# Deferring the table build, adding buffers, moving work between engines and re-ordering a linear-attention, Fourier-mix and MLP kernel

## The chip, the cores and the metric

The kernel runs on one core of one Trainium2 chip. The metric is the device time of one execution in microseconds (us). The kernel before took 268.16 us (median of three executions, 267.31 to 1089.49; the long one is a first execution and is not used; a fourth, 265.46, was taken with the changed kernel, and the median of the three fast ones is the 267.3 of the tables). Most fast executions of one kernel agree within about 1%. In a slow one the time is over 1.5% above the fastest of the same kernel.

Names: TensorE (PE in the profile, PEld for its weight loads), VectorE (DVE), ScalarE (ACT), GpSimd (POOL). Sync (SP) issues most DMAs. "Span" is the length of the profiled execution, some 2 us less than its time.

## The reference, cut to what matters

```python
B, H, S, D = 4, 8, 768, 48                    # d_model = H*D = 384, hidden = 1536
for t in range(S):                            # linear attention with a decaying state
    cur = einsum('bhd,bhe->bhde', u * k_t, v_t)
    y_t = einsum('bhd,bhde->bhe', r_t, state + cur)
    state = w_t[..., None] * state + einsum('bhd,bhe->bhde', k_t, v_t)
x = y, heads merged to (B, S, 384)
mixed = real(fft(fft(x, axis=1), axis=2))     # Fourier mix over both axes
u = x + mixed
un = (u - mean(u)) / sqrt(var(u) + 1e-6)
out = u + maximum(un @ w_ch1, 0) @ w_ch2      # two dense layers, the "experts" of this text
```

## The kernel before

The sequence is cut into six chunks of 128 positions per batch, 24 in all. Every chunk goes through Ln of the decay, matmuls for the running sums, Exp, products, transposes and matmuls, and lands in `x`. A "fold" on VectorE makes even and odd halves of `x`. The Fourier mix of a batch is matmuls of the folded `x` with cosine and sine tables, which the kernel builds itself, and then with a second table (`dtm`, `dtp`). After the mix come normalisation and the experts: `unt` x `w1`, relu to `ht`, then `ht` x `w2`.

No instruction stream is written by hand. Each operation is recorded with its engine, a duration in ns and a priority key. A list scheduler in Python then fixes the order of each engine's instructions. The order is static, so a wrong duration in the model gives another order on the chip.

```python
    def op(self, eng, dur, fn, r=(), w=(), key=None, sem=None, nbytes=0): ...   # cut
    # schedule(): of all ready operations, the one with the least (start, key, idx) goes next
    ...
    NIN = 3                                        # input buffers, 2 of most chunk buffers
    ...
        for i in range(2):                         # small_constants()
            op("dve", 600, fill(RH[i][:, :, :], 0.0), w=[("RH", i)])
            op("pool", 600, fill(XF[i][:, :, :], 0.0), w=[...])     # the whole of xf
        op("dve", 140, ts(MSK[:, :], CI[:, :], 0.0, None, ALU.is_gt), r=["CI"], w=["MSK"])
    ...
        for q in range(NC // 2):                   # seq_tables(): two scratch buffers in turn
            i = (q + 1) % 2
            ...                                    # range reduction on VectorE
            op("act", 420, act(SS[:, q, :], TF[i][:, :], ACTF.Sin, scale=sc), r=[("TF", i)], w=[("SS", q)])
            op("act", 420, act(CS[:, q, :], TG[i][:, :], ACTF.Sin, scale=-sc, bias=BHPI[:, :]),
               r=[("TG", i), "BHPI"], w=[("CS", q)])
    ...
        # attention(): the first use of Ln waits for the table set that has Ln and Exp
        op("act", 420, act(L[:, :, 0:D], wt[:, :, :], ACTF.Ln), r=["ACTT", ("in", "w", i3)], w=[("LB", i2)])
    ...
        op("dve", 270, tt(xf[:, c, 0:193], xb[:, c, 0:193], xb[:, c, 384:191:-1], ALU.add), ...)   # fold
        op("dve", 270, tt(xf[:, c, 321:512], xb[:, c, 1:192], xb[:, c, 383:192:-1], ALU.subtract), ...)
    ...
            op("dve", 270, ts(un[:, :], uf[:, kb, :], agg[:, kb, 0:1], None, ALU.subtract), ...)   # mix()
    ...
                if j % 3 == 2: ...                 # a third of the relus on VectorE, the rest on ScalarE
    ...
    T0, P = 30.0, 44.0                             # key windows: one for all the work of a batch
    def win(b):
        return (0.0, T0) if b == 0 else (T0 + (b - 1) * P, T0 + b * P)
    small_constants()
    seq_tables()
    dm_tables()
    op("act", 1300, lambda e: e.preload_act_table_set("natural_log_exp_and_others"),
       r=[("SS", 2), ("CS", 2), "DTM0", "TS", "DTM2"], w=["ACTT"])
```

## Time and profile before

| | before |
|---|---|
| time, median of the fast runs | 267.3 us |
| span of the profiled execution | 264.3 us |
| first TensorE work | 31.8 us |
| first expert matmul (`unt` x `w1`) | 90.0 us |
| from there to the end | 174.3 us |
| VectorE busy in all | 205.2 us |

The page of the profile gives busy time by engine, the span in 40 slices of 6.6 us (each digit is the busy share in tenths, 9 is 90% or more) and the chain of work that ended last, followed back from the end:

```profile
PE 200.9 (76%) x1776; PEld 125.3 (47%) x1776; DVE 205.2 (78%) x420; ACT 134.5 (51%) x291; POOL 108.6 (41%) x115
...
PE   0000197786785599999977899999778999969995
...
DVE  8999559368999996956899988568999774596232
...
DMA  6999496199792455522577853235410100100102
...
PE 45%; DVE 34%; SPq 8%; ACT 7%; DMA 2%; issue 2%; DVEq 0%; ACTq 0%
```

TensorE does nothing for almost five slices. After that neither engine is full: the chain changes between TensorE (45%) and VectorE (34%), so neither alone bounds the kernel. There is also a dip in the TensorE row four slices from the end.

The same in stretches, from the per-stretch busy times (start:end in us, length, busy us of each engine with its number of instructions, then granted TensorE clock, DMA share, GB/s):

```profile
0.00:31.80 31.80, 0.00 (x0) 0.00 (x0) 28.19 (x70) 9.56 (x16) 19.25 (x27) 1.00 0.92 158
31.80:72.00 40.20, 31.52 (x305) 21.25 (x305) 28.04 (x48) 26.09 (x56) 20.72 (x22) 0.83 0.76 149
72.00:90.00 18.00, 11.66 (x111) 6.50 (x112) 18.00 (x37) 9.79 (x24) 12.95 (x13) 1.00 0.52 102
90.00:264.30 174.30, 157.75 (x1361) 97.59 (x1361) 130.96 (x267) 89.03 (x197) 55.69 (x55) 1.00 0.34 78
```

Why TensorE waits is seen in the timeline (start, length, engine, line, operation, and in brackets how long the engine idled before and what released it):

```profile
2.00 2.65 POOL L386 MEMSET xf<- 128x3072 bf16 x1
...
2.50 2.23 DVE L379 TENSOR_SCALAR msk<-ci 128x128 bf16<-128x128 f32 x1
...
29.86 1.28 ACT L738 ACT_TABLE_LOAD   x1
31.23 0.94 ACT L389 ACTIVATE lb<-in_w 128x384 bf16<-128x384 f32 x2
...
31.81 0.50 PE L517 MATMUL bank<-lb,msk 128*128 128x384 bf16 x1 [31.81 <-ACT lb L389]
...
237.07 3.10 PE L696 MATMUL bank<-unt,w 128*128 128x384 bf16 x18 [0.58 <-ACT unt L677]
```

The first Ln (`lb`) stands behind the Sin evaluations and a table load, and TensorE waits 31.81 us for it. The last batch's experts start at 237.07, after a stretch in which its Fourier mix and normalisation ran alone. The `msk` comparison of 128 columns took 2.23 us beside a GpSimd memset of `xf` that took 2.65.

The groups by shape give the fold pieces and the mean subtraction (count, then busy us, mean ns of one, and idle time of the engine before them):

```profile
L375 DVE TENSOR_TENSOR xf<-x 128x191 bf16<-128x191 f32 x24 | 17.7, 739 | 0.0
...
L379 DVE TENSOR_SCALAR un<-uf,agg 128x384 bf16<-128x384 f32 x24 | 13.2, 552 | 0.0
...
L375 DVE TENSOR_TENSOR xf<-x 128x193 bf16<-128x193 f32 x24 | 10.3, 431 | 0.4
```

### The profile page before, as it was taken

How to read it: one execution, taken by the hardware profiler on the slowest of the kernel's cores; microseconds unless marked ns; L12 is line 12 of the kernel's file. 1: busy time of each engine (PE TensorE's matmuls, PEld its weight loads, DVE VectorE, ACT ScalarE, POOL GpSimd, SP SyncE). 2: the span in 40 equal slices, each digit the busy share in tenths (PEclk: the TensorE clock that was granted, in tenths of full speed). 3: DMA queues.
4: the chain of work that ended last, by engine and by line, in shares of the span. 5: the costliest groups of instructions: out<-in, count | busy, mean ns of one | idle time of the engine just before them, and what ended most of it. 6: DMA issues, size and time to landing. Idle time of an engine off the chain costs nothing.

```text
span 264.3 us, 4663 instructions
## 1 busy us (share of the span) xinstructions
PE 200.9 (76%) x1776; PEld 125.3 (47%) x1776; DVE 205.2 (78%) x420; ACT 134.5 (51%) x291; POOL 108.6 (41%) x115
## 2 busy tenths in 40 slices
PE   0000197786785599999977899999778999969995
PEld 0000165453543256665543566655435666536562
DVE  8999559368999996956899988568999774596232
ACT  1024584575673571745677717456767163227140
POOL 9940642358696458412264774122644200000000
PEclk9999999568899999999999999999999999999999
DMA  6999496199792455522577853235410100100102
GB/s 127 188 196 194 86 216 124 34 176 186 151 198 51 83 116 128 116 60 83 105 144 139 167 132 74 60 83 99 92 30 2 60 32 30 60 2 0 61 32 89
DMA packets 105478, 26.45 MB, mean 100 GB/s; under 512 B 100336, under 2 KB 105072, under 8 KB 105456
## 3 DMA queue, kind: packets, MB, share of 16 engines
q1 hardware_dynamic: 103440, 23.80, 42.7%
q0 software_dynamic: 2016, 2.36, 5.3%
q8 instruction: 14, 0.23, 0.4%
q14 instruction: 8, 0.07, 0.1%
HBM read 23.79 MB, written 4.72 MB: 108 GB/s over the span
## 4 chain that ended last, share of the span: by engine, by line
PE 45%; DVE 34%; SPq 8%; ACT 7%; DMA 2%; issue 2%; DVEq 0%; ACTq 0%
PE bank L715 16%; PE bank L696 11%; SPq L398 8%; DVE xf L375 6%; DVE ah L581 5%; DVE rh L375 5%; PE bank L639 4%; DVE bst L661 4%; DVE uf L657 4%; PE bank L577 4%; DVE un L379 3%; DVE x L614 3%; DMA in_v<-in_v_dram 2%; PE bank L558 2%; PE bank L606 2%
## 5 line engine op out<-in xcount | busy, mean ns | idle before, releaser
L696 PE MATMUL bank<-unt,w 128*128 128x384 bf16 x288 | 53.5, 326 | 1.5 <-ACT unt L677 1.0
L715 PE MATMUL bank<-w,ht 128*128 128x384 bf16 x288 | 51.7, 326 | 0.3 <-DVE ht L701 0.3
L705 ACT ACTIVATE ht<-bank 128x384 bf16<-128x384 f32 x64 | 31.5, 493 | 23.7 <-PE bank L696 23.6
L375 POOL TENSOR_TENSOR vtd<-in_v,dc 128x384 f32<-128x384 f32 x24 | 21.0, 876 | 54.0 <-DVE x L614 29.5
L715 PEld LDWEIGHTS bank<-w,ht 128*128 128x128 bf16 x288 | 27.1, 98 | 17.3 <-issue 1.3
L696 PEld LDWEIGHTS bank<-unt,w 128*128 128x128 bf16 x288 | 26.1, 98 | 17.2 <-ACT ht L705 1.0
L517 PE MATMUL bank<-lb,msk 128*128 128x384 bf16 x24 | 9.1, 380 | 33.1 <-ACT lb L389 32.8
L581 DVE TENSOR_TENSOR ah<-bank,msk 128x512 bf16<-128x512 f32 x48 | 31.1, 681 | 2.3 <-PE bank L577 2.2
L567 ACT ACTIVATE rtb<-bank 128x1024 bf16<-128x1024 bf16 x24 | 24.6, 1025 | 15.0 <-PE bank L558 15.0
L375 POOL TENSOR_TENSOR rk<-in_r,in_k 128x384 f32<-128x384 f32 x24 | 25.3, 1054 | 15.1 <-DMA in_r<-in_r_dram 14.7
L720 DVE SCALAR_TENSOR_TENSOR osb<-bank,rstd,uf 128x384 f32<-128x384 f32 x24 | 14.8, 615 | 21.1 <-PE bank L715 20.9
L375 POOL TENSOR_TENSOR rku<-rk,ub 128x384 f32<-128x384 f32 x24 | 26.3, 1099 | 0.3
L375 DVE TENSOR_TENSOR xf<-x 128x193 bf16<-128x193 f32 (+1 forms) x48 | 26.0, 585 | 0.4
L375 POOL TENSOR_TENSOR kh<-in_k,e_1 128x384 bf16<-128x384 f32 x12 | 13.1, 1090 | 24.3 <-ACT e_1 L625 11.4
L701 DVE TENSOR_SCALAR ht<-bank 128x384 bf16<-128x384 f32 x32 | 17.6, 550 | 6.8 <-PE bank L696 6.4
L389 ACT ACTIVATE vb<-in_v 128x384 bf16<-128x384 f32 x24 | 12.5, 521 | 15.7 <-PE bank L609 13.1
L577 PE MATMUL bank<-rtb,ktb 128*128 128x256 bf16 x96 | 16.6, 293 | 3.4 <-ACT ktb L569 1.7
L558 PE MATMUL bank<-idb,rh 128*128 128x128 bf16 x192 | 17.4, 246 | 1.9 <-DVE rh L375 1.8
L517 PEld LDWEIGHTS bank<-lb,msk 128*128 128x128 bf16 x24 | 2.5, 105 | 34.3 <-ACT lb L389 33.1
L569 ACT ACTIVATE ktb<-bank 128x512 bf16<-128x512 bf16 x24 | 14.3, 594 | 7.3 <-PE bank L564 7.1
L599 DVE TENSOR_TENSOR st<-bank,we 128x384 bf16<-128x384 f32 x20 | 11.0, 550 | 8.6 <-PE bank L594 8.4
L677 ACT ACTIVATE unt<-bank 128x384 bf16<-128x384 bf16 x24 | 11.8, 491 | 11.3 <-PE bank L672 11.2
(102 smaller groups left out, 409.9 us busy)
## 6 DMA issues: line engine op xcount, KB each, us to landing
in_w<-in_w_dram SPq DMA_DIRECT2D x24, 192.0 KB, 3.5
in_k<-in_k_dram SPq DMA_DIRECT2D x24, 192.0 KB, 3.6
in_r<-in_r_dram SPq DMA_DIRECT2D x24, 192.0 KB, 3.2
in_v<-in_v_dram SPq DMA_DIRECT2D x24, 192.0 KB, 3.1
out_dram<-osb SPq DMA_DIRECT2D x24, 192.0 KB, 1.9
w<-in_moe_w_ch_dram POOLq DMA_DIRECT2D x6, 384.0 KB, 9.5
ub<-in_u_dram SPq DMA_DIRECT2D x1, 192.0 KB, 3.7
```

Of the source, the lines that this page charges most:

```text
L375: return lambda e: e.tensor_tensor(out=o, in0=a, in1=b, op=f)
L398: return e.dma_start(INB[n][i][:, :, :], src[n][b, :, c * CH:(c + 1) * CH, :].rearrange("h t d -> t h d"))
L558: ins = e.transpose(psb(trr)[:, 128 * h:128 * h + 128], rflat[:, o0:o0 + 128], IDB[:, :])
L567: op("act", 910, lambda e: e.activation(rT[:, :, :].rearrange("p h t -> p (h t)"), psb(trr)[:, :], ACTF.Copy), r=[trr], w=[("RTB", i2)])
L569: op("act", 480, lambda e: e.activation(kT[:, :, :].rearrange("p h t -> p (h t)"), psb(trk)[:, 0:512], ACTF.Copy), r=[trk], w=[("KTB", i2)])
L577: ins = e.matmul(ps(ta)[:, 256 * x:256 * x + 256], kT[:, q, :], rT[:, 2 * q:2 * q + 2, :].rearrange("p h t -> p (h t)"))
L581: op("dve", 600, lambda e, hf=hf, ta=ta: e.tensor_tensor(out=ah[:, 4 * hf:4 * hf + 4, :], in0=ps(ta)[:, :].rearrange("p (h t) -> p h t", t ...
L696: ins = e.matmul(ps(t)[:, 0:384], W1[:, m, 128 * j:128 * j + 128], unt[:, m, :], start=(m == 0), stop=(m == NM - 1))
L701: op("dve", 480, lambda e, j=j, t=t, ht=ht: e.tensor_scalar(out=ht[:, j, :], in0=ps(t)[:, 0:384], scalar1=0.0, scalar2=None, op0=ALU.max), ...
L705: op("act", 380, lambda e, j=j, t=t, ht=ht: e.activation(ht[:, j, :], ps(t)[:, 0:384], ACTF.Relu), r=[t], w=[("HT", q % 2, j)])
L715: ins = e.matmul(ps(t)[:, 0:DM], ht[:, j, 128 * x:128 * x + 128], W2[:, j, :], start=(j == 0), stop=(j == NJ - 1))
L720: op("dve", 480, lambda e, kb=kb, t=t, o=o: e.scalar_tensor_tensor(out=o[:, :], in0=ps(t)[:, 0:DM], scalar=rstd[:, kb:kb + 1], in1=uf[:, k ...
```

## The change

The intent: let attention start at once and build the tables beside it, with all nine Sin evaluations in one visit to the Sin table set (three table loads in all; before had two). Give the scheduler more buffers, take work off VectorE, and give it new keys and durations that are nearer to those measured. The fold pieces are also laid out so that they start at even columns. Cut to its core:

```diff
-    NIN = 3
+    NIN = 5
+    NB = 3                                        # chunk buffers, 2 before; vb and vtd 4, 3 before
-        op("pool", 600, fill(XF[i][:, :, :], 0.0), ...)
+        op("pool", 400, fill(XF[i][:, :, 0:64], 0.0), ...)          # only the padding
+        op("pool", 400, fill(XF[i][:, :, 446:512], 0.0), ...)
+    def tables():
+        sins = []
+        ...                                        # same arithmetic on VectorE, one buffer per result
+        def all_sins(e):
+            for f in sins:
+                ins = f(e)
+            e.preload_act_table_set("natural_log_exp_and_others")
+            return ins
+        op("act", 8000, all_sins, r=[...], w=["DTM0", "DTM1", "DTM2"] + [...])
     def weights():
-            op("pool", 1000, ..., w=[("W1", q)], ...)
+            op("pool", 1000, ..., r=[("in", "v", 2)], w=[("W1", q)], ...)   # behind the third chunk's v
-        op("act", 420, act(L..., ACTF.Ln), r=["ACTT", ("in", "w", i3)], ...)
+        op("act", 500, act(L..., ACTF.Ln), r=[("in", "w", i3)], ...)
-        op("dve", 470, tt(rh...), ...)             # and so on for all durations
+        op("dve", 700, tt(rh...), ...)
-        op("dve", 270, tt(xf[:, c, 0:193], xb[:, c, 0:193], xb[:, c, 384:191:-1], ALU.add), ...)
+        op("dve", 350, tt(xf[:, c, 64:256], xb[:, c, 0:192], xb[:, c, 384:192:-1], ALU.add), ...)
-            op("dve", 270, ts(un[:, :], uf[:, kb, :], agg[:, kb, 0:1], None, ALU.subtract), ...)
+            op("dve", 100, ts(nmu[:, :], agg[:, kb, 0:1], -1.0, None, ALU.mult), ...)
+            op("act", 600, act(un[:, :], uf[:, kb, :], ACTF.Identity, bias=nmu[:, :]), ...)
-                if j % 3 == 2:                     # relu on VectorE
+                if j % 6 == 5:
-    T0, P = 30.0, 44.0
+    A0, AP, F0, FL, M0, ML, P, KT, KW = 39.3, 5.6, 23.3, 16.1, 48.9, 42.4, 44.9, 7.9, 13.3
+    # keys: attention, Fourier mix and experts of a batch have a window each; tables at KT
```

Smaller parts, not shown: the Exp of the state's decay is merged into a larger Exp on ScalarE, a GpSimd product is written in place, and the mix takes its parts in another order.

## The prediction

> **What bounds it now.** The span is 264.3 us. TensorE starts at 31.8 us: the waits show it idle until the first Ln, which stands behind the Sin tables and two table loads (1.28 us each). In 0 to 31.8 VectorE is busy 28.2 us and DMA 92%. Attention of batch 0 then runs to about 72 us, and the first expert matmul (unt x w1) starts at 89.9 us (timeline). From 72 to 90 VectorE is busy 18.0 of 18.0 us, TensorE 11.7: VectorE-bound. From 90 on TensorE is busy 157.8 of 174.3 us, VectorE 131 (per-stretch busy times); the period is about 49 us (last batch's first expert matmul at 237.1). "Busy" overstates TensorE: spacings in the timeline (162 ns for 384 columns, about 56 ns for a transpose, 25 ns for 48 columns) sum to about 180 us, 45 per batch, against 200.9 busy. From 230 to 237 us the last batch's Fourier step and normalisation stand alone.
>
> **Costs.**
> - Start: Ln waits only for its input and one table load, so TensorE starts near 6 us. Not all 26 us come home: about 18 us of table arithmetic on VectorE (sum of its uncontended durations) moves into attention of batch 0, which takes 28 us of VectorE itself; six input chunks take 4.4 us of DMA each, and 14 us of weights now come in among them. VectorE ends batch 0's attention at about 48 us. I expect the first expert matmul at 60 us (55 to 67), 30 us sooner.
> - The big memsets of xf (2.65, 2.94 us on GpSimd) shrink. Beside them VectorE's msk, nle and ta took 2.2, 2.2 and 2.9 us. The Trainium skill ("SBUF — State Buffer", Who interferes with whom) calls the port pair that these engines share an exclusive lock; the trace agrees in kind.
> - Mean subtraction: 13.2 us leave VectorE, 3.4 return (24 negations); ScalarE gets about 12.5. Relu: 16 pieces move, 8.8 us off VectorE, 7.9 onto ScalarE. ScalarE loses the we exponentials (3.6) and gains a table load (1.3).
> - Even-aligned fold: nothing by itself. Both pieces take about 0.36 us alone; the 0.74 mean of the second is waiting beside GpSimd, which x releases. That stays.
> - Totals: VectorE 205 to about 180, ScalarE 134 to 152, GpSimd 108 to 104, TensorE unchanged. Per batch: TensorE 45, VectorE 38, ScalarE 36. TensorE becomes the clear bound.
> - Third chunk buffers, five inputs, new order: period from 49 to about 47 us; the last batch's Fourier step goes under the previous batch's expert matmuls, saving some 5 us.
>
> **Sum.** 60 us, then 153 us of remaining TensorE work at about 91% density (86% before, from 90 us) = 168: span 228, time about 231 us. Range 220 to 244. Faster by over 2%: 0.97; within 2%: 0.02; slower: 0.01.
>
> **Right or wrong.** Right: first TensorE work before 9 us; three table loads, Sin in one visit; first unt x w1 at 55 to 67; later TensorE busy share at least 93%; VectorE 174 to 186 us; fold pieces with unchanged mean beside GpSimd; no TensorE hole over 2 us before the last batch's experts.
>
> **What would make it wrong.** The Sin visit (about 8 us of ScalarE in program order) waits for VectorE's last table operand, so late VectorE stalls all attention; weights crowd out chunks 3 to 5; the static order, set by modelled times, stalls engines; GpSimd lock waits grow, VectorE being denser early; a lower granted clock (0.83 in 31.8 to 72) over a longer early stage.

## The result, and the profile after

| | before | after | predicted |
|---|---|---|---|
| time, median of the fast runs | 267.3 us | 237.69 us (237.35 to 238.53) | 231 (220 to 244) |
| ratio of fast runs, 95% interval | | 0.891, 0.884 to 0.897 | |
| span | 264.3 | 235.8 | 228 |
| first TensorE work | 31.8 | 6.1 | before 9 |
| first expert matmul | 90.0 | 72.2 | 60 (55 to 67) |
| from there to the end | 174.3 | 163.6 | 168 |
| VectorE busy | 205.2 | 185.5 | 174 to 186 |
| ScalarE busy | 134.5 | 153.1 | 152 |

Ratios here and below are the mean time of one kernel's fast runs over that of the other's in the same rounds, so they are not quite the ratio of the quoted medians. Two of the four executions had a mean granted clock of 0.92 and two of 0.985, and they took the same time (237.99 and 237.38 against 237.35 and 238.53), so a difference in clock of that size shows no cost here.

The page after:

```profile
PE 200.0 (85%) x1776; PEld 130.1 (55%) x1776; DVE 185.5 (79%) x403; ACT 153.1 (65%) x316; POOL 105.0 (45%) x118
...
PE   0765475549769999999998999899989999999994
...
DVE  8999999398998389999769998894899866822222
...
DMA  6999999989970559852365678104200000020102
...
PE 63%; DVE 19%; DMA 9%; ACT 5%; issue 2%; SPq 1%; DVEq 0%; ACTq 0%
```

TensorE is full from the thirteenth slice (5.9 us each) to the end, and the dip near the end is gone. In the first twelve slices it is half idle, while VectorE and DMA are at eight or nine in nearly all of them. The chain has DMA in it now, 9% of the span. The stretches say the same:

```profile
0.00:72.00 72.00, 43.01 (x360) 27.48 (x361) 66.39 (x148) 41.81 (x78) 47.93 (x60) 0.77 1.00 187
72.00:120.00 48.00, 47.26 (x431) 30.32 (x429) 38.98 (x87) 36.38 (x81) 24.04 (x26) 0.95 0.54 116
120.00:164.00 44.00, 41.91 (x410) 28.02 (x408) 38.84 (x81) 33.15 (x72) 23.65 (x24) 1.00 0.47 102
164.00:209.00 45.00, 44.15 (x439) 30.28 (x437) 34.73 (x78) 32.02 (x68) 9.40 (x9) 1.00 0.11 34
209.00:235.80 26.80, 23.67 (x146) 14.04 (x144) 6.56 (x11) 9.77 (x20) 0.00 (x0) 1.00 0.15 54
```

From 72 us on TensorE is busy 157.0 of 163.8 us (the sum of the last four lines), 96%, against 90.5% before. In the first 72 us VectorE is busy 66.4 us and the DMA share is 1.00. The timeline:

```profile
6.05 0.48 PE L525 MATMUL bank<-lb,msk 128*128 128x384 bf16 x1 [6.05 <-ACT lb L389]
...
43.58 1.28 ACT L389 ACT_TABLE_LOAD   x1
44.88 0.53 ACT L389 ACTIVATE ss<-uf 128x385 bf16<-128x385 f32 x1
...
49.28 1.28 ACT L488 ACT_TABLE_LOAD   x1
50.58 0.60 ACT L575 ACTIVATE ktb<-bank 128x512 bf16<-128x512 bf16 x1
...
58.65 2.24 DVE L375 TENSOR_TENSOR xf<-x 128x192 bf16<-128x192 f32 x2
...
72.24 1.17 PE L708 MATMUL bank<-unt,w 128*128 128x384 bf16 x3
```

The visit to Sin is one piece of 7.0 us (43.58 to 50.58). The fold at 58.65 is that of batch 0's sixth chunk: VectorE ends batch 0's attention at 60.9 us. The groups by shape:

```profile
L375 DVE TENSOR_TENSOR xf<-x 128x191 bf16<-128x191 f32 x24 | 15.7, 655 | 0.0
...
L389 ACT ACTIVATE un<-uf,nmu 128x384 bf16<-128x384 f32 x24 | 14.1, 605 | 0.0
...
L375 DVE TENSOR_TENSOR xf<-x 128x192 bf16<-128x192 f32 x24 | 12.7, 530 | 0.1
...
L379 DVE TENSOR_SCALAR nmu<-agg 128x1 f32<-128x1 f32 x24 | 3.4, 141 | 0.0
```

The chain of waits in the first 75 us holds one piece far longer than any other (start, length, what):

```profile
22.94 1.83 SPq L398
24.82 16.01 DMA in_v<-in_v_dram
40.85 0.52 ACT vb L389
```

The v of the sixth chunk took 16.0 us from issue to landing, where the median v took 3.5. The six weight loads (2.36 MB) are issued on GpSimd's queue from 22.6 us on, just around it. The Trainium skill states this ("DMA: Bandwidth & Descriptors", Issuing engines are not separate DMA queues): DMAs of all issuers run on the same 16 engines and interleave. The trace agrees: the v is issued by Sync and the weights by GpSimd, and when the weights come later (weights_late below) the same v lands in 4.5 us.

So the time is as predicted, but not its parts. The first stage gave 17.8 us and not 30, and what follows it gave 10.7 us and not 6. Two questions remain: what holds the first stage at 72 us, and which part of the change shortened the rest?

### The profile page after: what moved, and what is told of

It is laid out like the page before. It is cut to its first block, busy times and chain, and to the rows that moved or that the text cites. A ratio compares the mean times of both kernels' runs of the same rounds, so it can differ in the third digit from the quotient of the medians.

```text
span 235.8 us, 4671 instructions
## 1 busy us (share of the span) xinstructions
PE 200.0 (85%) x1776; PEld 130.1 (55%) x1776; DVE 185.5 (79%) x403; ACT 153.1 (65%) x316; POOL 105.0 (45%) x118
## 3 DMA queue, kind: packets, MB, share of 16 engines
q0 software_dynamic: 2016, 2.36, 5.9%
## 4 chain that ended last, share of the span: by engine, by line
PE 63%; DVE 19%; DMA 9%; ACT 5%; issue 2%; SPq 1%; DVEq 0%; ACTq 0%
PE bank L727 19%; PE bank L708 18%; DMA in_v<-in_v_dram 7%; DVE xf L375 6%; PE bank L648 6%; PE bank L664 5%; PE bank L564 3%; PE bank L583 3%; DVE rh L375 3%; DVE ah L587 3%; DVE x L620 2%; PE bank L684 2%; DMA in_w<-in_w_dram 2%; PE bank L612 2%; PE bank L570 1%
## 5 line engine op out<-in xcount | busy, mean ns | idle before, releaser
L708 PE MATMUL bank<-unt,w 128*128 128x384 bf16 x288 | 58.0, 333 | 0.0
L717 ACT ACTIVATE ht<-bank 128x384 bf16<-128x384 f32 x80 | 37.9, 500 | 19.2 <-PE bank L708 19.0
L375 DVE TENSOR_TENSOR xf<-x 128x192 bf16<-128x192 f32 (+1 forms) x48 | 26.6, 593 | 0.1
L375 POOL TENSOR_TENSOR rk<-rk,ub 128x384 f32<-128x384 f32 x24 | 25.2, 1051 | 1.3
L375 POOL TENSOR_TENSOR kh<-in_k,e_0 128x384 bf16<-128x384 f32 x8 | 8.8, 1096 | 31.3 <-ACT e_0 L538 31.3
L564 PEld LDWEIGHTS bank<-idb,rh 128*128 128x128 bf16 x192 | 13.7, 108 | 11.8 <-DVE rh L375 8.5
L612 PE MATMUL bank<-vb,ah 128*128 128x48 bf16 x192 | 15.8, 189 | 5.0 <-DVE ah L587 4.9
L713 DVE TENSOR_SCALAR ht<-bank 128x384 bf16<-128x384 f32 x16 | 8.8, 552 | 12.6 <-PE bank L708 12.6
L612 PEld LDWEIGHTS bank<-vb,ah 128*128 128x128 bf16 x192 | 13.1, 100 | 9.5 <-DVE ah L587 6.5
L389 ACT ACTIVATE lb<-in_w 128x384 bf16<-128x384 f32 x24 | 12.5, 523 | 5.9 <-DMA in_w<-in_w_dram 5.9
```

The lines of the kernel that those rows point to most:

```text
L375: return lambda e: e.tensor_tensor(out=o, in0=a, in1=b, op=f)
L564: ins = e.transpose(psb(trr)[:, 128 * h:128 * h + 128], rflat[:, o0:o0 + 128], IDB[:, :])
L612: ins = e.matmul(ps(ty)[:, D * h:D * h + D], ah[:, h, :], vb[:, h, :], start=True, stop=first)
L708: ins = e.matmul(ps(t)[:, 0:384], W1[:, m, 128 * j:128 * j + 128], unt[:, m, :], start=(m == 0), stop=(m == NM - 1))
L717: op("act", 475, lambda e, j=j, t=t, ht=ht: e.activation(ht[:, j, :], ps(t)[:, 0:384], ACTF.Relu), r=[t], w=[("HT", q % 2, j)])
```

## The experiments

Theories for the first stage: **V**, VectorE holds it, because the table arithmetic (some 18 us) is now among attention's own work; **W**, the weight loads among the input loads hold it. Rivals to both are the static order and the waits of VectorE at GpSimd. The quoted expectations call them by these letters or in words. For what follows the first stage, the rivals are the relief of VectorE, the buffers, and the work order. All times are medians of fast runs (three rounds, four executions, unless said otherwise). "Stretch" is the profiled span less the start of the first expert matmul. All runs gave the right result unless one is called wrong.

### weights_late: weights behind the sixth chunk, order otherwise kept

```diff
+    late = [o for o in pool if o.sem and o.sem[0] == "w"]     # the weight DMAs on GpSimd
+    v5 = [o for o in g.ops if o.sem == "in_v0"][1]            # v of the sixth chunk
+    # after the schedule is made: taken out, made to wait for v5, put before the sixth rk
```

> The changed kernel, every engine's order kept, with the six weight loads moved behind the last input chunk of batch 0. Question: why did the first expert matmul start at 72.2 us and not at the forecast 60. Theory W (the weights crowd out the inputs: the load of v of the sixth chunk took 16 us, 24.8 to 40.8): that load lands in under 7 us, the first expert matmul comes at 64 to 67 us, time 230 to 233 us. Theory V (VectorE's volume, table arithmetic and attention with its waits at the port shared with GpSimd, sets it; VectorE is busy 66.4 of the first 72 us): only the 3.5 us VectorE gap at 41 us closes, first expert matmul not before 69 us, time 234 to 238 us.

Measured: 236.18 us (234.68 to 237.27), ratio to before 0.886 (0.880 to 0.891). The first expert matmul is at 71.7 us and the stretch 163.4. The long DMA has left the chain (the v lands in 4.5 us), and nothing clear was gained. Its place in the chain is filled by many pieces of VectorE and GpSimd:

```profile
34.00 1.35 DVE uf L384
...
37.82 1.14 POOL vtd L376
```

The time from 24 to 41 us, in which the changed kernel waits for that v, shows why. The first line is the changed kernel, the second weights_late (the third busy time is VectorE's):

```profile
24.00:41.00 17.00, 10.13 (x76) 6.31 (x75) 17.00 (x33) 6.51 (x13) 12.80 (x14) 0.50 1.17 191
24.00:41.00 17.00, 12.30 (x111) 8.43 (x108) 17.00 (x38) 12.66 (x23) 11.74 (x12) 1.00 1.05 205
```

VectorE is busy all the time in both. So W alone fails.

### no_tables: the table arithmetic cut to 8 columns (wrong result)

```diff
-            op("dve", 350, ts(TQ[0][:, :], KI[:, :], TN[:, q:q + 1], MAGIC, ALU.mult, ALU.add), ...)
+            op("dve", 350, ts(TQ[0][:, 0:8], KI[:, 0:8], TN[:, q:q + 1], MAGIC, ALU.mult, ALU.add), ...)
             # and so on; the Sin evaluations keep their size and read KI instead
```

> The changed kernel, order kept, with the table arithmetic on VectorE cut to 8 columns (wrong result on purpose; the Sin visit stays). Theory V: some 12 to 15 us of VectorE work leave the first 40 us, the first expert matmul comes at 60 to 65 us, time 226 to 231 us. Theory W: the v load of the sixth chunk still lands near 40 us and holds attention; first expert matmul at 69 us or later, time 234 to 238 us.

Measured: 237.66 us, 0.892 (0.888 to 0.897), first expert matmul at 72.1. VectorE's busy time in the first 41 us fell by 9.3 us (40.02 to 30.75), less than the 12 to 15 expected; 3.9 us came back before 72 us, so it lost 5.0 us in all (180.5). The time didn't move, so V alone fails as well. From 24 to 41 us VectorE now has room (8.98 us busy of 17.00), but the chain waits for DMA, this time for a w:

```profile
23.91 15.42 DMA in_w<-in_w_dram
39.35 0.53 ACT lb L389
```

```profile
24.00:41.00 17.00, 6.74 (x54) 4.35 (x52) 8.98 (x19) 5.29 (x10) 10.44 (x11) 0.50 1.19 200
```

### both_lifted: the two together (wrong result)

> The changed kernel, order kept, with both suspected limits of the first stage lifted at once: weights behind the sixth chunk, and the table arithmetic cut to 8 columns (wrong result on purpose). Each alone left the first expert matmul at 72 us. If the loads and VectorE are two limits of nearly the same length: now 60 to 67 us, time 225 to 232 us. If neither limits it and the chain after 46 us (static order, GpSimd waits) does: 70 us or later, time 234 us or more.

The edit is the sum of the last two. Measured: 228.54 us (228.02 to 229.59), 0.863 (0.858 to 0.867). Batch 0's sixth fold ends at 51.5 us, the first expert matmul is at 62.7 us and the stretch is unchanged at 163.5:

```profile
50.89 0.61 DVE L376 TENSOR_TENSOR xf<-x 128x192 bf16<-128x192 f32 x2
...
62.67 1.17 PE L709 MATMUL bank<-unt,w 128*128 128x384 bf16 x3
```

Each cut alone gave nothing beyond the noise; together they gave 9.4 us of the first stage (72.1 in no_tables to 62.7). Two limits of nearly equal length lie side by side there, and the slower one hides the other. The order of the instructions was kept in all three, but for the weight loads, so a fixed order cannot be what holds 72 us. The DMA share in the first 62 us is 1.04 to 1.07 in the changed kernel and in all three, so the share doesn't tell whether attention waits for DMA; the chain does.

### pool_light: GpSimd's products on one head of eight (wrong result)

```diff
-        op("pool", 1050, tt(rk[:, :, :], rt[:, :, :], kt[:, :, :], ALU.mult), ...)
+        op("pool", 1050, tt(rk[:, 0:1, :], rt[:, 0:1, :], kt[:, 0:1, :], ALU.mult), ...)
         # the same for rku, vtd and kh; the rest of their tiles is zeroed once
```

> The changed kernel, order kept, with GpSimd's four products per chunk cut to one head of eight (wrong result on purpose). It measures what VectorE's waits beside GpSimd cost. Forecast: both fold pieces fall from 0.53 and 0.66 us to 0.35, the products rh from 0.84 to 0.55, VectorE's busy total from 185.5 to 160 to 167 us. If those waits matter to the time (theory V includes them): first expert matmul at 62 to 67 us, time 227 to 232 us. If they hide under TensorE or the loads: time 234 us or more.

Measured: 228.4 us, 0.857 (0.853 to 0.861). VectorE does the same instructions in 159.7 us, 25.8 less than after, with GpSimd at 42.4 us:

```profile
L375 DVE TENSOR_TENSOR xf<-x 128x191 bf16<-128x191 f32 x24 | 9.0, 375 | 0.0
L375 DVE TENSOR_TENSOR xf<-x 128x192 bf16<-128x192 f32 x24 | 8.6, 357 | 0.1
```

The two fold pieces, 655 and 530 ns after, take 375 and 357 ns when GpSimd is quiet. So some 10.8 of the 28.4 us that the profile calls VectorE's busy time in the fold are waiting beside GpSimd. The first expert matmul is at 68.5, just outside the 62 to 67 forecast for the case that the waits matter, and the stretch is 158.0. Only 3.7 us come in the first stage, where the DMA limit still stands (a load of r takes 14.95 us in its chain). The run has a second effect: shorter products also shorten the paths through GpSimd, so it bounds what the waits cost from above and doesn't measure them alone.

### tables_first: all tables before attention, all else as after

```diff
-    g.key = KT
+    g.key = -1.0
-        ..., r=[("in", "w", i3)], ...)             # Ln
+        ..., r=["DTM0", ("in", "w", i3)], ...)
```

> The changed kernel with the tables put back in front: the first Ln waits for the Sin visit, all else as changed (the scheduler orders anew). If the early start of attention is worth what the prediction said (first expert matmul earlier by the table time less what VectorE gives back): TensorE starts at 22 to 28 us, first expert matmul at 82 to 90 us, time 248 to 256 us. If the gain came mainly from the new order and the lighter VectorE after the start: under 243 us.

Measured: 243.68 us, 0.914 (0.909 to 0.918); first TensorE work at 32.0 us, first expert matmul at 78.5, stretch 163.9. The time lies between the two cases of the expectation, just above the second. Undoing the deferral costs 6 us, although TensorE starts 26 us later.

### defer_only: the kernel before, with only the deferred tables and the one Sin visit

```diff
-    TF = [... for i in range(2)]                   # and TG
+    TF = [... for i in range(6)]
-            op("act", 420, act(SS[:, q, :], TF[i][:, :], ACTF.Sin, scale=sc), ...)
+            sins.append(act(SS[:, q, :], TF[q][:, :], ACTF.Sin, scale=sc))   # one operation for all
-        op("act", 420, act(L..., ACTF.Ln), r=["ACTT", ("in", "w", i3)], ...)
+        op("act", 420, act(L..., ACTF.Ln), r=[("in", "w", i3)], ...)
```

> The kernel before with one part of the change alone: the table arithmetic runs while attention runs, all Sin in one visit, so the first Ln waits only for its input. Putting the tables back in front of the changed kernel cost only 6 us, with the first TensorE work 26 us later. If the early start alone is worth about that much, because the loads and VectorE then hold batch 0: TensorE starts near 6 us, first expert matmul at 80 to 88 us, time 256 to 263 us. If the early start would be worth its 26 us in the kernel before, with its fewer buffers and early weights: time 240 to 248 us.

Measured: 264.94 us against 266.1 of before, 0.997 (0.992 to 1.002). TensorE starts at 5.68 us and the first expert matmul comes at 83.9, 6 us sooner; the stretch after it grows from 174.3 to 177.8 us. The first expert matmul came as expected and the time did not (256 to 263). The most visible part of the change gives almost nothing on its own. Why the stretch grows was not followed up.

### balance_back and buffers_back: VectorE's relief undone, the buffers undone

```diff
-                if j % 6 == 5:
+                if j % 3 == 2:                     # balance_back; and un on VectorE again
```

> The changed kernel with the mean subtraction on VectorE again and every third relu there (not every sixth). VectorE's busy total should go from 185.5 to 195 to 205 us, ScalarE's from 153 to 130 to 135. If VectorE's load holds the expert stretch: it grows from 163.6 to 168 us or more, time 241 to 248 us. If TensorE alone bounds it and hides the difference: 235 to 240 us.

Measured: 236.58 us, 0.887 (0.883 to 0.892), first expert matmul at 72.4, stretch 162.9. VectorE is back at 199.5 us and the time is that of after.

```diff
-    NIN = 5
-    NB = 3
+    NIN = 3                                        # buffers_back; vb and vtd 3 as well
+    NB = 2
```

> The changed kernel with three input sets and two chunk sets as before. If deeper buffers let batch 0's loads run ahead and chunks overlap: the first expert matmul moves from 72 to 78 us or later, time 241 to 250 us. If loads and VectorE limit batch 0 whatever the buffers: 71 to 75 us, time 236 to 240 us.

Measured: 236.56 us, 0.889 (0.885 to 0.892), first expert matmul at 74.5, stretch 161.2. Undoing the buffers costs nothing either. In both runs the scheduler made the order anew, so each shows the part together with the order that goes with it.

### old_keys: after, with before's key windows

```diff
-    A0, AP, F0, FL, M0, ML, P, KT, KW = 39.3, 5.6, 23.3, 16.1, 48.9, 42.4, 44.9, 7.9, 13.3
+    T0, P = 30.0, 44.0                             # one window per batch, KT and KW kept
```

> The changed kernel with the work order of before: its priority windows (30 and 44 us), all else as changed. If the order is the main cause of the 10.8 us gained after the first expert matmul (163.6 instead of 174.4 us): that stretch takes 170 us or more, the TensorE hole before the last batch's experts (230 to 237 us in before) is back, time 244 to 254 us. If balance and buffers are the cause: 235 to 241 us.

Measured: 251.76 us, ratio of fast runs 0.946 (0.941 to 0.952). The first execution was slow, and it is the profiled one, so its parts are not compared here. The times of the fast ones (250.93 to 253.48) are some 14 us above after's: this small edit of keys costs more than undoing the deferral, the balance or the buffers.

### old_durs: after, with the scheduler told before's durations

```diff
+        dur = {("act", 500): 420, ("act", 470): 375, ("dve", 700): 470, ...}.get((eng, dur), dur)
```

> The changed kernel with the scheduler told the durations of before (ScalarE and VectorE too short, the 48-column matmul groups twice too long), keys as changed. If the corrected durations carry the order: stretch after the first expert matmul 170 us or more, time 243 us or more. If the keys carry it: 235 to 241 us.

Measured: 252.73 us (252.52 to 253.09), 0.954 (0.950 to 0.958), first expert matmul at 74.5, stretch 176.2. Nothing the chip executes differs except the order of the instructions. The lighter VectorE, the buffers, the fold layout and the small merges are all in this kernel, and its stretch is no shorter than before's (174.3): without the order they shorten nothing there. So the new keys don't carry the gain without the durations they were made with.

### order_only: new keys and durations, the other parts undone

```diff
     # tables_first + balance_back + buffers_back, and weights neither gated nor late (KW = 6.0)
```

> The new work order alone (its keys and the scheduler's measured durations), everything else of the change undone: tables in front, three input and two chunk sets, weights loaded at once, mean subtraction and every third relu on VectorE; the folded layout and small merges stay. So far neither balance nor buffers alone moved the time, the old keys cost 15 us, the early start 6 us. If the order is the cause of the shorter expert stretch: from the first expert matmul on it takes 160 to 167 us (174.4 in before), first expert matmul at 80 to 90 us, time 246 to 256 us. If it needs the lighter VectorE or the buffers as well: the stretch is 170 us or more, time 257 us or more.

Measured: 252.16 us, 0.952 (0.947 to 0.958), first TensorE work at 35.96 us, first expert matmul at 84.8, stretch 165.0. The stretch is that of after, with VectorE at 196.7 us. The fold layout and the small merges of after are still in this kernel, so they are not separated from the order here; old_durs shows that they don't shorten the stretch without it.

With tables_first the first stage can be read as a staircase. The first expert matmul goes from 90.0 us (before) to 84.8 (order_only: the order with the layout and the merges), 78.5 (tables_first) and 72.2 (after). The two middle runs differ in the balance, the buffers and the later weights, and the three together take 6.3 us off the first stage and the time from 252.16 to 243.68 us (other rounds; ratios 0.952 and 0.914), although balance and buffers, each undone alone in the changed kernel, cost no time. No run undoes the later weights by themselves, so it may be they alone; this was not tested.

### both_right: both limits lifted with a right result

```diff
-        ...                                        # five VectorE operations for the sign table alt
+        op("pool", 450, lambda e: e.iota(ALT2[:, :], [[0, (HF + 1) // 2], [-2, 2]], base=1, ...))
-            op("dve", 490, fill(RH[i][:, :, :], 0.0), ...)
+            op("pool", 1100, fill(RH[i][:, :, :], 0.0), ...)
-            op("dve", 550, stt(TG[q]..., -1.0, ..., ALU.mult, ALU.max), ...)
+            op("act", 530, act(TG[q][:, :], TF[q][:, :], ACTF.Abs), ...)
-            op("dve", 350, ts(q, a, -float(DM), None, ALU.mult), ...)
-            op("dve", 550, stt(f, ki, MC[:, j:j + 1], q, ALU.mult, ALU.add), ...)
+            op("act", 530, act(f, ki, ACTF.Identity, scale=MC[:, j:j + 1]), ...)
+            op("dve", 550, stt(f, a, -float(DM), f, ALU.mult, ALU.add), ...)
-               r=[("in", "v", 2)], w=[("W1", q)], ...)
+               r=[("in", "v", 0)], w=[("W1", q)], ...)            # behind the sixth chunk's v
```

> The changed kernel with both limits of its first stage lifted, with a right result: the weight loads wait for the v of the sixth chunk; the alternating sign table is made on GpSimd without arithmetic, two memsets of rh move to GpSimd, the absolute values and the products k*m of the tables move to ScalarE, where there is room. About 7 us leave VectorE, so VectorE is busy 176 to 180 us in all. The work order is made anew with these durations, so it isn't the same order. If the two limits are what holds the first stage (theory both limits), the first expert matmul comes at 63 to 67 us and the time is 228 to 233 us, as in the wrong-result run that lifted both. If it is the fixed order and the waits on GpSimd for the rest (rival), or if the moved work only moves the queue to ScalarE and GpSimd, the first expert matmul stays at 70 us or later and the time at 234 us or above.

Measured: 234.78 us (234.44 to 237.5), 0.884 (0.878 to 0.891), first expert matmul at 70.6, stretch 162.1. The case of the two limits failed, and both numbers lie where its rival was put (70 us or later, 234 us or above). VectorE has 13 instructions fewer, but is busy 184.8 us, not 176 to 180; in the first 72 us it is busy 66.3 us, as it was after (66.4), while GpSimd rose from 47.9 to 52.1. The timeline shows how one saving was given back:

```profile
7.40 2.23 POOL L433 IOTA alt<- 128x386 bf16 x1
7.59 2.25 DVE L383 TENSOR_SCALAR ht<-ki,tn 128x385 f32<-128x385 f32 x1
```

The sign table that left VectorE is made on GpSimd in 2.23 us, and beside it a VectorE operation, whose like took 0.42 us at 6.68 us in after, took 2.25. As in weights_late, no DMA is in the chain of the first stage. The DMA limit is lifted and VectorE's is not. As the order was made anew here, it isn't excluded as a part of the cause. The time can't be told from that of weights_late, so no version with a right result that clearly beats the changed kernel was found.

## Why the prediction was right or wrong

**The time: right.** 237.7 against 231, inside the range. The mechanism was right in outline: work starts at 6 us, the stretch after the first stage is bound by TensorE, and the hole before the last batch's experts is gone. Part of the nearness is luck: the first stage ended 12.2 us too late and the rest took 4.4 us less than predicted, which partly cancels, and the gain in the rest was put down to the wrong parts (below).

**"I expect the first expert matmul at 60 us (55 to 67), 30 us sooner": wrong, and the largest miss.** It came at 72.2, 17.8 us sooner. The step that failed is "VectorE ends batch 0's attention at about 48 us": it ended at 60.9. The 12 us that the prediction left from there to the first expert matmul were right (11.3). It had added some 28 us of attention to 18 us of table arithmetic, the latter at durations measured without contention, 46 in all. VectorE was busy 55.3 of the 60.9 us (constants included), and the wait of 16.0 us for inputs behind the weights ran beside it as a second limit. The prediction named both ("14 us of weights now come in among them"), and its list of what would make it wrong had "weights crowd out chunks 3 to 5" and "GpSimd lock waits grow, VectorE being denser early". The runs show the first in the 16.0 us, and the second as a bound: with GpSimd's products cut (pool_light) VectorE is busy 54.4 of the first 72 us and not 66.4. both_lifted ends the attention at 51.5 and puts the first expert matmul at 62.7, so the two limits hold about 9.4 of the 12.2 us missed. That run goes without work that the predicted 60 included, so it doesn't confirm the 60, and the rest of the miss is not explained.

**"Not all 26 us come home": right, and too mild.** The deferral is worth 6 us of 26 with the new order (tables_first) and about 1 us of time in the kernel before (defer_only, not clear of zero; the interval reaches to 2.3 us), because TensorE's early idle time was not what held the first stage.

**The period and the last batch: right in kind, wrong in cause.** The stretch after the first expert matmul was predicted at 168 and is 163.6, from 174.3. The prediction led with "TensorE becomes the clear bound" from moving work off VectorE, and gave the period 49 to 47 us to buffers and order together (it went from 49.0 to 45.6). balance_back gives VectorE 14 us back, buffers_back takes the buffers away, and neither costs anything (stretch 162.9 and 161.2). Going back to the old keys or to the old durations costs 14 and 15 us, and order_only keeps the short stretch (165.0) with the rest undone. The order does it, and it needs both its keys and its durations. The fold layout and the small merges don't give it alone (old_durs has them, with a stretch of 176.2); what they add to the order was not separated.

**Even-aligned fold: right.** The pieces changed from 431 and 739 ns to 530 and 655, the sum over all 48 from 28.0 to 28.4 us (10.3 + 17.7, 12.7 + 15.7). In pool_light, with GpSimd quiet, they take 357 and 375. What they lose is lost beside GpSimd.

**Smaller points: right.** First TensorE work at 6.1 us; three table loads; VectorE 185.5; TensorE busy 96% after the first stage; no hole before the last experts (202 to 209.1 us: busy 7.1 of 7.1). That last point was a weak test: in the kernel before, TensorE was busy 4.7 of 7.1 us there (230 to 237.1), in several gaps of under 1 us each, so the hole was worth about 2.4 us and not 5, and no single gap was over 2 us there either. The large memsets went and `msk` fell from 2.23 to 0.55 us.

**Open.** What the waits at GpSimd cost by themselves: pool_light bounds them, with the shorter paths through GpSimd, at about 9 us. Which of balance, buffers and later weights the first stage needs (6.3 us between order_only and tables_first).

## What to carry to other kernels

When a stage has two limits of nearly equal length, cutting either alone shows nothing, and each such run looks like proof that it didn't matter: cut both before discarding either. An engine's later start is worth only what the stage's true limit lets through, so find that limit before counting idle time as gain. Where a static scheduler makes the order, the durations it is told are part of the kernel, and moving work from VectorE to GpSimd can come back as waiting on VectorE.

## What the Trainium skill lacked or had wrong

- "ScalarE: Activation LUTs", What ACT_TABLE_LOAD costs, gives about 1.283 us for the load and 1.38 us for a drain. The trace has loads of 1.28 us, and no drain beside them: the load at 43.58 starts 0.01 us after the record before it ends (`ktb`, 42.97 to 43.57), and the Sin that follows starts 0.02 us after it ends. Here a switch costs 1.3 us, half of what the page says.
- The same section's formula for an ACTIVATE with one pointer operand (186 + 93 + 0.833 x 384, an estimate of 599 ns) needs no correction: `un` took 605 ns.
- "SBUF — State Buffer", Who interferes with whom, names tensor_scalar among the VectorE operations that can take the port pair shared with GpSimd, and says that the other engine then blocks fully. The trace agrees in kind: an iota on GpSimd, which reads no tile, took 2.23 us and the tensor_scalar beside it 2.25. What the section lacks is what such waits add up to in a kernel: here up to 25.8 of VectorE's 185.5 busy us (after less pool_light).
- "Vector Engine (DVE) Microarchitecture Reference", Performance modes — why throughput varies by op and dtype, says that 4-byte alignment makes no difference, for forms other than this one (fp32 inputs, two sources, bf16 output). The fold adds this form: the piece whose output started at column 321 before and at 256 after took 343 ns at its shortest in both, and the kernel gained nothing.
- "Perfetto Trace Analysis", Identifying the Most-Contended Engine, says to optimise the engine with the highest occupancy first (DMA it judges by HBM utilization instead). Among the engines that was VectorE in the first 72 us (66.4 us), and cutting its work (no_tables) gained nothing until the weights were moved as well (both_lifted). The section has no word on limits that tie.
- No page says what a static order is worth. Here the same instructions in another order took 252.7 us instead of 237.7.
